# Mamba-2 scan and an ELU layer pair on one core: the first two blocks' second layer half in seven products

## Chip, cores, metric

One core of one Trainium2 chip runs the program. The metric is the device time of one execution in microseconds (us); for the kernel before it is the median of three runs, 355.29 us (355.22 to 355.34).

## The reference

All of it is float32. First a chunked state-space scan (Mamba-2 SSD) for 4 batches and 8 heads over 768 tokens, head size 32, state size 16; its output is laid out as 3072 tokens by 256 features and goes through two dense layers with an ELU between:

```python
# per chunk of tokens: cum = running sum of log(a)
M = (C @ B.T) * exp(cum_i - cum_j) * causal
y = M @ x + (C @ state) * exp(cum_i)
state = exp(sum) * state + B.T @ (x * exp(cum_last - cum_j))
...
h = x @ w_in                                  # (3072, 256) @ (256, 2048)
g = np.where(h > 0.0, h, np.exp(np.minimum(h, 0.0)) - 1.0)
out = g @ w_out                               # (3072, 2048) @ (2048, 256)
```

The weights arrive as float64 and are made into float32 words on the chip.

## The kernel before, in words

The 3072 tokens are cut into twelve blocks of 256 (`BLK`), numbered n = 0 to 11. Blocks 2k and 2k+1 form a pair: the same third of the sequence, in two batches. For every block the scan makes `yT` (features on partitions, tokens along the free axis). The first layer, `l1(n, i)`, makes 256 of the 2048 features (two chunks j of 128, index m = 2i + j) in one PSUM bank; `elu` turns that into a tile `g_of[n, i]` of 128 x 2 x 256: ScalarE does relu(-h) and the exponential, VectorE the last step. The second layer sums over m = 0 to 15 in PSUM.

From block 4 on, pairs go through both layers by Strassen's scheme in Winograd's form: a 2x2 block product by seven products instead of eight, for sums and differences of quarters. In layer one these are `front`, `mid` and `back` (products at L733) with `sum_y` (four differences of `yT`, GpSimd, L728). In layer two it is the generator `second(n)` (L820 to L900), which takes the pair n, n+1 in two halves of four indices i. Each `next` of it issues two products of 128 columns (L856); after each of the seven products a few operations follow: copies by ScalarE (L863, L875), additions into `c_sum` (`add`: by VectorE where an operand is in PSUM, else by GpSimd, L834), and in-place subtractions on the quarters of g (`sub`, GpSimd, L798). The operands are named as in the scheme: b11, b21, b12, b22 are quarters of g (`quarters`), t1 = b12 - b11 is put in b12's place (`sum_t1`, L810), t2 = b22 - t1 goes into a tile of its own (`sum_t2`). The weights have sums too: for each index i, `weight_steps` (L703) makes s3 = a11 - a21, then a21 + a22 in place, s2 and s4, for `w_in` (`s_in`) and for `w_out` (`s_out`).

In the kernel before, blocks 2 and 3 go through layer one plainly and through layer two by `second(2)`. Blocks 0 and 1 go through both layers plainly: `l2(n, j)` (L775) does, for the features m = 2j and 2j+1, one product of 256 columns for each of two halves of the tokens (L782), and behind the last one ScalarE copies the sum into the tile `ob` (L788), which is stored (L790).

The order of the work is written out by hand; every engine runs its own instructions in the program's order, and semaphores join them. The parts in order:

- a start-up, in which the scan of blocks 0 and 1, the first weights and `l1(0, 0..3)` are done;
- twelve steps s (L1040): `l1` of blocks 1 and 0 in turn, with the scan of block 2 and five pieces of the weights put in between (`w_take`: ScalarE and VectorE; `w_give`: VectorE, and GpSimd at L239);
- loops `n = 2` and `n = 3` (L1164), eight steps i each: `l2(n - 2, i)` and `l1(n, i)`, with the scans of blocks 3, 4 and 5 (`scan_ahead`, `turn_part`, `end_of_two`), the last pieces of the weights (n = 2), and the sums of the weights with t1 of block 2 (n = 3, `more_sums`, L1158). At i = 6 of `n = 3`, `across` and `inside` finish the scan of blocks 4 and 5 and `sum_y(4)` follows;
- loops n = 4, 6, 8, 10 over pairs: `front`, `mid`, `back` of pair n between the steps of `second(n - 2)`;
- `second(10)` alone.

A block's matrix of C is masked by heads in `mask_heads(n)` (L452, one VectorE operation of 128x512), between the transposes (`turn_square`, VectorE, L447) and `scores`. PSUM has seven buffers of one bank for everything (`ps_a`) and one for sums (`ps_o`). `c_sum`, the tile that collects the output of a pair, has one buffer, and so has the scratch `p_sum`; g has twelve buffers for even and twelve for odd n; t2 has four. All output and nearly all input goes through SP's DMA queue.

Of the kernel before, what the change touches and what calls it, by code (L numbers as in the profile page):

```python
# [16 lines left out]
P = 128  # L17
# [11 lines left out]
def kernel(  # L29
# [422 lines left out]
    def mask_heads(n):  # L452
        s = st[n]
        s["ctm"] = att.tile([P, 2, 2, P], F32, tag="ctm", name="ctm")
        nc.vector.tensor_tensor(
            out=s["ctm"], in0=s["ct"].unsqueeze(2).to_broadcast([P, 2, 2, P]),
            in1=hmask2.unsqueeze(1).unsqueeze(3).to_broadcast([P, 2, 2, P]), op=ALU.mult)
# [194 lines left out]

    def l1(n, i, parts=1):

        ps = psum([P, 2, BLK], "ps_h")
        for j in range(2):
            m = 2 * i + j
            for part in range(parts):
                toks = slice(part * BLK // parts, (part + 1) * BLK // parts)
                for k in range(KC):  # L660
                    nc.tensor.matmul(  # L661
                        out=ps[:, j, toks], lhsT=w_in[:, k, m * P:(m + 1) * P],
                        rhs=yT[n // 2][:, k, n % 2].rearrange("p u i -> p (u i)")[:, toks],
                        start=(k == 0), stop=(k == KC - 1))
        lag.append((n, i, ps))
# [107 lines left out]
    o_of = {}  # L773

    def l2(n, j, half=None):  # L775


        if j == 0 and half != 1:
            o_of[n] = p_o.tile([P, 2, DM], F32, tag="o", name="ps_o")
        for m in (2 * j, 2 * j + 1) if half is None else (2 * j + half,):  # L780
            for ts in range(2):
                nc.tensor.matmul(  # L782
                    out=o_of[n][:, ts], lhsT=g_of[n, j][:, m % 2, ts * P:(ts + 1) * P],
                    rhs=w_out[:, m], start=(m == 0 and ts == 0), stop=(m == MC - 1),
                    skip_group_check=True)
        if j == MC // 2 - 1 and half != 0:
            ob = ffn.tile([P, 2, DM], F32, tag="ob", name="ob", bufs=1)
            nc.scalar.copy(out=ob, in_=o_of.pop(n))  # L788
            r0 = row_of(n)
            nc.sync.dma_start(  # L790
                out=out[r0:r0 + BLK, :].rearrange("(t p) e -> p t e", p=P), in_=ob)
# [5 lines left out]
    def sub(out, in0, in1):  # L797
        nc.gpsimd.tensor_tensor(out=out, in0=in0, in1=in1, op=ALU.subtract)  # L798

    def quarters(n, i):  # L800


        A, B = g_of[n, i], g_of[n + 1, i]
        if n < 4:
            return A[:, 0], A[:, 1], B[:, 0], B[:, 1]
        return A[:, 0], B[:, 0], B[:, 1], A[:, 1]
# [5 lines left out]
    def sum_t2(n, half):  # L812
        for i in range(4 * half, 4 * half + 4):
            t2_of[n, i] = ffn.tile([P, BLK], F32, tag="t2", name="t2", bufs=4)
            b11, b21, b12, b22 = quarters(n, i)
            sub(t2_of[n, i], b22, b12)

    c_of = {}

    def second(n, last=False):  # L820


        c = c_of[n] = ffn.tile([P, 2, 2, 2, P], F32, tag="c", name="c_sum", bufs=1)
# [3 lines left out]
        for half in range(2):  # L827
# [8 lines left out]
            for r, a in enumerate((a11, a12, s1, s2, s3, a22, s4)):  # L836
# [25 lines left out]
                if r == 0:  # L862
                    nc.scalar.copy(out=p1, in_=ps)  # L863
                    for i in chunk:
                        b11 = quarters(n, i)[0]
                        sub(b11, t2_of[n, i], b11)
                    if half:
                        add(c11, c11, p1)
# [171 lines left out]
    for s, (n, i) in enumerate((  # L1040
            (1, 0), (1, 1), (1, 2), (0, 4), (1, 3), (0, 5), (1, 4), (0, 6), (1, 5), (0, 7),
            (1, 6), (1, 7))):
        l1(n, i, parts=2 if s < 2 else 1)
# [54 lines left out]
    def scan_ahead(n, i):  # L1098
# [29 lines left out]
        if 4 <= m < NP and n % 2 == 1:  # L1128
            if i == 0:
                scaled(m, nc.gpsimd)  # L1130
                scaled(m + 1, nc.gpsimd)
            for k in (i,) if m == 4 else (i, i + 1) if i % 2 == 0 else ():
# [25 lines left out]
    def more_sums(i):  # L1158
        sum_weights(nc.vector, a_out, s_out, i)
        sum_weights(nc.gpsimd, a_in, s_in, i)  # L1160
        sum_t1(2, i, nc.vector)


    for n in (2, 3):  # L1164
        for i in range(8):
            if n == 3 and i > 0:
                more_sums(i - 1)
            l2(n - 2, i)
            piece = todo < len(pieces) and (n, i) != (2, 1)
            if n == 2 and i == 0:  # L1170
                elu()
            if piece:
                w_take(todo, nc.scalar if i > 1 else nc.vector)
# [12 lines left out]
            if n == 2:  # L1186
# [3 lines left out]
                if i == 1:  # L1190
                    scores(3)
                    sums(3)
                    for q in range(4):
                        weigh(3, q)
                if i == 2:
                    states(3)
                if i == 6:
                    inside(across(3), 3)
            else:
                if i == 0:  # L1200
                    s_in[:], s_out[:] = weight_sums(), weight_sums()
            scan_ahead(n, i)
            end_of_two(n, 2 * i + 1)
    sum_t2(2, 0)
    left = weight_steps(nc.vector, a_out, s_out, 7)

    for n in range(4, NP, 2):
# [14 lines left out]
        for k in range(16):  # L1222
            i = k // 2
            if k % 2 == 0:
# [12 lines left out]
                else:  # L1237
                    front(n, i)
                    front_sums(n, i)
                    next_elu()  # L1240
                    l2s(2)
# [11 lines left out]
            else:  # L1253
                mid(n, i)
                if i == 0 and n > 4:
# [9 lines left out]
                if n == 4 and i < 4:  # L1265
                    next(left)()
                    if i == 0:
                        sum_weights(nc.gpsimd, a_in, s_in, 7)
                        sum_t1(2, 7)
# [45 lines left out]
```

## Time and profile before

| | us |
|---|---|
| median of three runs | 355.29 |
| the profiled execution | 354.71 |
| its span in the profile | 352.9 |
| TensorE busy | 346.8 (98% of the span) |
| VectorE busy | 240.5 (68%) |
| GpSimd busy | 231.7 (66%) |
| ScalarE busy | 204.2 (58%) |

The profile is of one execution; its span begins with the first instruction seen and ends with the last. PE is TensorE (PEld its weight loads, which run beside its products), DVE VectorE, ACT ScalarE, POOL GpSimd, SP the engine that issues most DMAs. A line of a timeline reads: start, duration, engine, line of the code, operation, output tile <- input tiles, shape, and in brackets the idle time just before it and what ended it. Consecutive instructions of one kind are merged, with their count behind "x"; the durations of TensorE's records overlap, so the cost of one is read from the start of one group to the start of the next. Costly groups of the work that the change touches:

| group | count | mean ns |
|---|---|---|
| L782 TensorE, layer two plain, 128x256 (two records a product) | 128 | 382 |
| L856 TensorE, seven products, 128x128, w_out with g (two records a product) | 640 | 275 |
| L455 VectorE, mask of C, 128x512 | 9 | 922 |
| L798 GpSimd, subtraction, 128x256 (three groups) | 120 | 730 to 752 |
| L810 GpSimd / VectorE, t1, 128x256 | 33 / 7 | 727 / 488 |
| L834 GpSimd, add, 128x256 | 30 | 725 to 728 |
| L834 VectorE, add from PSUM, 128x256 | 59 | 417 to 422 |
| L709 GpSimd, a step of the sums of w_in, 128x128 | 32 | 490 to 528 |
| L709 VectorE, a step of the sums of w_out, 128x128 | 32 | 433 to 469 |
| L728 GpSimd, a difference of yT, 128x256 | 16 | 734 to 752 |

### The profile page before, as it was taken

What the parts mean: (1) busy time and instruction counts of PE and PEld (TensorE: products, weight loads), DVE (VectorE), ACT (ScalarE), POOL (GpSimd) and SP (SyncE); (2) the same over time, 40 slices, a digit from 0 to 9 for tenths busy, and PEclk for the clock granted to TensorE, in tenths of its full rate; (3) what the DMA queues carried; (4) which work ended last, traced back from release to release, by engine and by line L of the source; (5) the groups of instructions that cost most, each with busy time, mean ns of one, the idle gap of its engine ahead of it and who ended that gap; (6) DMA issues with size and microseconds to landing.
All of it is one profiled execution on the core that took longest, in us unless ns stands there. A gap on an engine that the chain in (4) does not pass through costs nothing.

```text
span 352.9 us, 9967 instructions
## 1 busy us (share of the span) xinstructions
PE 346.8 (98%) x3958; PEld 312.8 (89%) x3958; DVE 240.5 (68%) x500; ACT 204.2 (58%) x496; POOL 231.7 (66%) x368
## 2 busy tenths in 40 slices
PE   8889999999999999999999999999999999999996
PEld 5568888888888999999999999999999999999996
DVE  4998979863999768684777684677684565656212
ACT  5869989787335677536677535586635444435100
POOL 5654554553576996887377788468687545465883
PEclk9999999999999999999999999999999999999999
DMA  8979988641450500155500145600000100000001
GB/s 148 255 195 258 230 196 213 133 74 32 82 128 7 115 1 2 19 112 119 115 0 2 15 93 124 134 3 0 2 2 4 60 3 0 2 0 32 31 2 59
DMA packets 72726, 26.49 MB, mean 75 GB/s; under 512 B 57768, under 2 KB 67560, under 8 KB 72680
## 3 DMA queue, kind: packets, MB, share of 16 engines
q1 hardware_dynamic: 70360, 25.60, 31.8%
q8 instruction: 31, 0.51, 0.6%
q10 hardware_dynamic: 2320, 0.26, 0.5%
q14 instruction: 15, 0.12, 0.1%
HBM read 22.51 MB, written 3.34 MB: 73 GB/s over the span
## 4 chain that ended last, share of the span: by engine, by line
PE 95%; DVE 3%; ACT 1%; POOL 0%; issue 0%; DVEq 0%; POOLq 0%
PE ps_o L856 35%; PE ps_h L733 28%; PE ps_h L661 14%; PE ps_o L782 8%; PE ps_y L629 2%; PE ps_g L535 2%; PE ps_y L610 1%; PE ps_st L565 1%; PE ps_idle L254 1%; DVE g L683 1%; PE ps_o L842 1%; DVE M L544 0%; DVE mag L229 0%; ACT L L505 0%; PE ps_x L475 0%; PE ps_x L494 0%
## 5 line engine op out<-in xcount | busy, mean ns | idle before, releaser
L674 ACT ACTIVATE e<-ps_h 128x512 f32<-128x512 f32 x96 | 57.1, 594 | 91.3 <-DVE ps_h L758 49.3
L856 PEld LDWEIGHTS ps_o<-w_out,g 128*128 128x128 f32 x640 | 79.9, 192 | 2.9
L856 PE MATMUL ps_o<-w_out,g 128*128 128x128 f32 x640 | 80.9, 275 | 0.0
L683 DVE SCALAR_TENSOR_TENSOR g<-e,ps_h 128x512 f32<-128x512 f32 x96 | 65.1, 680 | 14.3 <-ACT e L681 13.7
L681 ACT ACTIVATE e<-e 128x512 f32<-128x512 f32 x96 | 60.9, 635 | 2.0
L661 PE MATMUL ps_h<-yT,w_in 128*128 128x256 f32 (+1 forms) x272 | 60.3, 370 | 1.1 <-POOL w_in L239 0.5
L810 POOL TENSOR_TENSOR g<-g 128x256 f32<-128x256 f32 x33 | 24.0, 727 | 54.9 <-DVE g L683 54.8
L661 PEld LDWEIGHTS ps_h<-yT,w_in 128*128 128x128 f32 x272 | 48.5, 190 | 8.4 <-POOL w_in L239 1.5
L515 ACT ACTIVATE L<-L,ncum 128x64 f32<-128x64 f32 x160 | 41.1, 338 | 0.2
L856 PE MATMUL ps_o<-w_sum,g 128*128 128x128 f32 x304 | 39.9, 275 | 0.0
L856 PEld LDWEIGHTS ps_o<-w_sum,g 128*128 128x128 f32 x304 | 38.5, 192 | 1.1
L766 DVE TENSOR_TENSOR ps_h<-ps_h,u_sum 128x512 f32<-128x512 f32 x32 | 22.3, 698 | 24.0 <-PE ps_h L733 23.7
L733 PE MATMUL ps_h<-yT,w_in 128*128 128x256 f32 x128 | 38.5, 383 | 0.0
L733 PE MATMUL ps_h<-y_sum,w_in 128*128 128x256 f32 x128 | 38.1, 380 | 0.0
L733 PE MATMUL ps_h<-y_sum,w_sum 128*128 128x256 f32 x128 | 38.1, 379 | 0.0
L520 POOL TENSOR_SCALAR_AFFINE_SELECT L<-L 64x512 f32<-64x512 f32 x40 | 28.0, 700 | 12.0 <-ACT L L515 10.7
L750 DVE TENSOR_TENSOR u_sum<-ps_h,u_sum 128x512 f32<-128x512 f32 x32 | 22.1, 690 | 15.1 <-ACT u_sum L743 11.0
L758 DVE TENSOR_TENSOR ps_h<-ps_h,u_sum 128x256 f32<-128x256 f32 x32 | 13.8, 433 | 25.6 <-PE ps_h L733 25.4
L782 PE MATMUL ps_o<-w_out,g 128*128 128x256 f32 x128 | 30.7, 382 | 0.0
L798 POOL TENSOR_TENSOR t<-g 128x256 f32<-128x256 f32 x40 | 28.8, 751 | 0.2
L798 POOL TENSOR_TENSOR g<-g,t 128x256 f32<-128x256 f32 x40 | 28.8, 752 | 0.3
L798 POOL TENSOR_TENSOR g<-t,g 128x256 f32<-128x256 f32 x40 | 27.9, 730 | 1.1 <-PE ps_o L856 1.1
(121 smaller groups left out, 536.9 us busy)
## 6 DMA issues: line engine op xcount, KB each, us to landing
L<-flat SPq DMA_DIRECT2D x20, 256.0 KB
w<-in_moe_w_out_dram SPq DMA_DIRECT2D x8, 512.0 KB
w<-in_moe_w_in_dram SPq DMA_DIRECT2D x7, 512.0 KB
xr<-in_x_dram SPq DMA_DIRECT2D x24, 128.0 KB
out_dram<-c_sum SPq DMA_DIRECT2D x9, 256.0 KB
bc<-in_B_dram SPq DMA_DIRECT2D x24, 64.0 KB
bc<-in_C_dram SPq DMA_DIRECT2D x22, 64.0 KB
ec<-flat_exp SPq DMA_DIRECT2D x10, 128.0 KB
```

Source lines behind the costliest of these rows:

```text
L515: nc.scalar.activation(L[:, h, u], L[:, h, u], ACT.Exp, bias=ncum[:, u, row:row + 1])
L520: nc.gpsimd.affine_select(out=part, in_=part, pattern=[[0, 4], [0, 2], [1, Q]], compare_op=ALU.is_ge, fill=0.0, base=0, channel_multiplier=-1)
L661: nc.tensor.matmul(out=ps[:, j, toks], lhsT=w_in[:, k, m * P:(m + 1) * P], rhs=yT[n // 2][:, k, n % 2].rearrange("p u i -> p (u i)")[:, toks],
L674: nc.scalar.activation(begun[0], lag[0][2], ACT.Relu, scale=-1.0)
L681: nc.scalar.activation(e, e, ACT.Exp, scale=-1.0)
L683: nc.vector.scalar_tensor_tensor(out=g_of[n, i], in0=e, scalar=1.0, in1=ps, op0=ALU.subtract, op1=ALU.max)
L733: nc.tensor.matmul(out=out, lhsT=lhsT, rhs=rhs, start=first, stop=True, skip_group_check=True)
L766: nc.vector.tensor_tensor(out=c2, in0=c2, in1=u[:, 0:2], op=ALU.add)
L782: nc.tensor.matmul(out=o_of[n][:, ts], lhsT=g_of[n, j][:, m % 2, ts * P:(ts + 1) * P], rhs=w_out[:, m], start=(m == 0 and ts == 0), stop=( ...
L798: nc.gpsimd.tensor_tensor(out=out, in0=in0, in1=in1, op=ALU.subtract)
L810: eng.tensor_tensor(out=b12, in0=b12, in1=b11, op=ALU.subtract)
L856: nc.tensor.matmul(out=ps[:, ts], lhsT=b[:, ts * P:(ts + 1) * P], rhs=a[:, i], start=(i == chunk[0] and ts == 0), stop=(i == chunk[-1]), s ...
```

## The change

Blocks 0 and 1 are made ready for the seven products in the second half of layer two (features 1024 to 2047, m = 8 to 15).

- In the twelve steps, `l1(1, 0..3)` come first, and the features i = 4 to 7 of both blocks are made together by `l1_two`: one product of 512 columns (both blocks' tokens) for each k. `g_of[0, i]` then holds the features 2i of both blocks and `g_of[1, i]` the features 2i + 1, and `quarters` reads them so.
- `l2` sums only m = 0 to 7 (four steps for each block, all in loop `n = 2`); ScalarE copies the sum into `c_sum` instead of `ob`. The second half runs as `second(0)`, with its second half alone, in loop `n = 3`: four `next` a step for i < 4, then three. Blocks 0 and 1 are stored from `c_sum` in loop 4.
- t1 (`sum_t1(0, 4..7)`) and t2 of these blocks are made by GpSimd in loop `n = 2`; after product one, two of the four subtractions go to VectorE.
- The sums of `w_out` for i = 4 to 7 move to loop `n = 2`, those for 0, 1, 2 stay in `n = 3`, those for 3 follow at the start of loop 4 (VectorE as before). Of the sums of `w_in` (GpSimd), the first step of each i goes to loop `n = 2` (`in_first`), the other three stay in `n = 3` (`in_rest`). `sum_t2(2, 0)`, which stood behind loop `n = 3`, now follows product five of `second(0)`.
- `scaled` of blocks 4 and 5 moves from the start of loop `n = 3` to the end of `n = 2`; both `decay` steps of block 5 in loop 3 come at i = 0.
- The masks of C from block 4 on are two ScalarE activations of 128x256 with a scale by partition, instead of one VectorE operation.

```diff
     def mask_heads(n):
...
+        if n > 3:
+            for k in range(2):
+                nc.scalar.activation(
+                    s["ctm"][:, :, k], s["ct"], ACT.Copy, scale=hmask2[:, k:k + 1])
+            return
...
+    def l1_two(i, j):
+        ps = psum([P, 2, BLK], "ps_h")
+        for k in range(KC):
+            nc.tensor.matmul(
+                out=ps, lhsT=w_in[:, k, (2 * i + j) * P:(2 * i + j + 1) * P],
+                rhs=yT[0][:, k].rearrange("p n u i -> p n (u i)"),
+                start=(k == 0), stop=(k == KC - 1))
+        lag.append((j, i, ps))
...
-        if j == MC // 2 - 1 and half != 0:
-            ob = ffn.tile([P, 2, DM], F32, tag="ob", name="ob", bufs=1)
-            nc.scalar.copy(out=ob, in_=o_of.pop(n))
...
+        if j == MC // 4 - 1:
+            if n == 0:
+                c_of[0] = ffn.tile([P, 2, 2, 2, P], F32, tag="c", name="c_sum", bufs=1)
+            nc.scalar.copy(
+                out=c_of[0][:, n].rearrange("p t e c -> p t (e c)"), in_=o_of.pop(n))
...
-        if n < 4:
+        if n == 2:
             return A[:, 0], A[:, 1], B[:, 0], B[:, 1]
+        if n == 0:
+            return A[:, 0], B[:, 0], A[:, 1], B[:, 1]
...
-        for half in range(2):
+        for half in range(2) if n else (1,):
...
                     nc.scalar.copy(out=p1, in_=ps)
+                    if not n:
+                        add(c11, c11, p1)
                     for i in chunk:
                         b11 = quarters(n, i)[0]
-                        sub(b11, t2_of[n, i], b11)
+                        sub(b11, t2_of[n, i], b11, nc.vector if n == 0 and i < 6 else nc.gpsimd)
...
-    for s, (n, i) in enumerate((
-            (1, 0), (1, 1), (1, 2), (0, 4), (1, 3), (0, 5), (1, 4), (0, 6), (1, 5), (0, 7),
-            (1, 6), (1, 7))):
-        l1(n, i, parts=2 if s < 2 else 1)
+    for s in range(12):
+        if s < 4:
+            l1(1, s, parts=2 if s == 0 else 1)
+        else:
+            l1_two(s // 2 + 2, s % 2)
...
+    steps = second(0)
     for n in (2, 3):
         for i in range(8):
-            if n == 3 and i > 0:
-                more_sums(i - 1)
-            l2(n - 2, i)
...
+            if n == 2:
+                l2(i // 4, i % 4)
...
+            else:
+                for _ in range(4 if i < 4 else 3):
+                    next(steps)
...
+                if i == 0:
+                    sum_t1(0, 4)
+                    sum_t1(0, 5)
...
+                if i in (3, 4):
+                    sum_t1(0, i + 3)
...
+                if i > 4:
+                    sum_weights(nc.vector, a_out, s_out, i - 1)
                 if i == 6:
+                    sum_weights(nc.vector, a_out, s_out, 7)
                     inside(across(3), 3)
+                if i in (5, 6):
+                    t2(0, 2 * i - 6)
+                    t2(0, 2 * i - 5)
+                    in_first(2 * i - 10)
+                    in_first(2 * i - 9)
+                if i == 7:
+                    for k in range(4, 8):
+                        in_first(k)
+                    scaled(4, nc.gpsimd)
+                    scaled(5, nc.gpsimd)
             else:
-                if i == 0:
-                    s_in[:], s_out[:] = weight_sums(), weight_sums()
+                if i > 0:
+                    in_rest(i - 1)
+                    sum_t1(2, i - 1, nc.vector)
+                if i in (1, 4, 6):
+                    sum_weights(nc.vector, a_out, s_out, (1, 4, 6).index(i))
...
-    sum_t2(2, 0)
-    left = weight_steps(nc.vector, a_out, s_out, 7)
+    left = weight_steps(nc.vector, a_out, s_out, 3)
...
-                if i == 0 and n > 4:
+                if i == 0:
                     store(n - 4, 0)
                     store(n - 4, 1)
...
-                if n == 4 and i < 4:
+                if n == 4 and i == 0:
                     next(left)()
-                    if i == 0:
-                        sum_weights(nc.gpsimd, a_in, s_in, 7)
-                        sum_t1(2, 7)
+                    next(left)()
+                    in_rest(7)
+                    sum_t1(2, 7)
```

## The prediction

> **What bounds the kernel now.** I read the page's slices first, then its chain of work that ended last, then the busy time by stage, then the rows of the two engines that meet where the change ends.
>
> ```profile
> PE   8889999999999999999999999999999999999996
> POOL 5654554553576996887377788468687545465883
> PEclk9999999999999999999999999999999999999999
> ...
> PE 95%; DVE 3%; ACT 1%; POOL 0%; issue 0%; DVEq 0%; POOLq 0%
> ```
>
> The granted clock is full in every slice, and the chain is TensorE. The second view gives busy time by stage; per engine it is us and, in brackets, instructions. My cuts are the twelve steps of blocks 0 and 1, loop `n = 2`, loop `n = 3`, loop `n = 4`, and the rest.
>
> ```profile
> 27.20:51.70 24.50, 24.49 (x285) 21.19 (x286) 21.75 (x46) 22.34 (x57) 12.70 (x17) 1.00 0.98 225
> 51.70:82.60 30.90, 30.90 (x294) 26.56 (x293) 22.82 (x44) 26.50 (x66) 15.16 (x19) 1.00 0.58 135
> 82.60:114.70 32.10, 32.10 (x434) 27.81 (x433) 27.10 (x63) 15.48 (x35) 20.85 (x40) 1.00 0.30 69
> 114.70:168.70 54.00, 54.00 (x644) 50.24 (x643) 37.50 (x78) 32.22 (x82) 45.15 (x73) 1.00 0.30 62
> ```
>
> The first two numbers are the stretch and TensorE's busy time: they are equal, so from 27 us on TensorE never stands still, and its waits in that stretch come back empty. Two things follow. A product taken away shortens the program in full, as long as nothing new makes TensorE wait; and relief on VectorE, ScalarE or GpSimd is worth nothing by itself. In loop `n = 3` (third line) VectorE is the busiest of the others (27.10), GpSimd (20.85) still has 11 us free.
>
> **TensorE's own work.** Prices come from TensorE's timeline and chain; each product of the code leaves two records there. Eight products of 128 columns ("PE ps_o L856 x16") take 1.78 us, 0.2225 each; four of 256 columns ("PE ps_o L782 x8") take 1.73 us, 0.432 each. A narrow product thus costs 51.5% of a wide one.
> - Second halves of layer two: 32 products of 256 go (two blocks, m = 8 to 15, two token halves), 13.82 us. In come 7 products x 4 chunks x 2 token halves = 56 of 128: 12.46 us. Gain 1.36.
> - `l1_two`: 32 products of 256 become 16 of 512. From the two prices, 0.0132 us of a product is fixed and the rest goes by columns, so this saves 16 x 0.0132 = 0.21. The one 512-column row is the idle product at 1.1 us, among rows at over twice today's price (512 and 384 columns took 3.35 us there), and measures nothing of this stream. Bounds 0 (columns alone count) and 0.42 (twice the fixed part); I take 0.21.
> - `parts=2` at the second of the twelve steps goes: 8 x 0.2225 - 4 x 0.432 = 0.05.
>
> Sum 1.62 us less on TensorE. A rule speaks against this: the Trainium skill, "TensorE: Matmul & The Clock Gate", section "Back-to-back issue gap", gives about 81 ns for a sustained matmul of 128 columns with its weight load and 131 for 512, so narrow ones are dear. By a straight line between these (an estimate from that page) 256 columns take 98 ns, and with two records to a product 56 narrow ones would cost 9.1 us against 6.3 for the 32 wide ones: a loss of 2.8. The trace has 111 and 216 ns per record in this very stream, and decides.
>
> **GpSimd's new work, and where it meets TensorE.** GpSimd gets for blocks 0 and 1: four t1, four t2, two of the four subtractions after product one (VectorE has the other two), four after product two, and five adds of 128x256. It loses nothing: the sums of `w_in` are only cut in two, the first of each four steps (`in_first`) now in `n = 2`, the other three (`in_rest`) in `n = 3`. So 19 operations at 0.70 (spacing of consecutive ones, four in 2.78) come in between 52 and 114 us, 13.3 us, and with them the four t2 of block 2, which used to stand behind loop `n = 3`. All of these lie ahead of one thing that TensorE needs: `sum_y(4)`, whose second result is the operand of the second product of `front(4, 0)`.
>
> ```profile
> 111.58 0.73 POOL L728 TENSOR_TENSOR y_sum<-yT 128x256 f32<-128x256 f32 x1 [2.20 <-ACT yT L646]
> 112.80 0.85 POOL L728 TENSOR_TENSOR y_sum<-yT,y_sum 128x256 f32<-128x256 f32 x1 [0.48 <-ACT yT L646]
> ...
> 114.55 0.59 PE L733 MATMUL ps_h<-yT,w_in 128*128 128x256 f32 x2
> 114.98 0.59 PE L733 MATMUL ps_h<-y_sum,w_sum 128*128 128x256 f32 x2
> ```
>
> GpSimd now waits 2.20 us for ScalarE's copies and is done at 113.65, 1.33 us before the product at 114.98. That is the whole cover. Afterwards, with the gain, the product is due at 114.98 - 1.62 = 113.36. I count GpSimd forward in its new order:
> - To the states' products `Sx`: the last weight piece is joined at 75.1 (0.6 later, since ScalarE's copy of block 0's half sum, 0.57, now precedes the later pieces). Behind it stand its own 1.24, four t2 2.8, eight `in_first` 3.4 to 4.2, two `scaled` 1.2, six selects 4.2, one add 0.7, six subtractions 4.2, two `in_rest` 2.9 to 3.5: done at 96.3 to 97.8. `Sx` is then released by VectorE, now at 98.38, afterwards near 98.7 (one t1 of 0.41 moves ahead of it, TensorE is 0.1 ahead): covered by 0.9 us or more, and `Sx` ends at 100.5.
> - From there: three adds 2.2, one more 0.7, four t2 2.8; four `in_rest`. A set of four such steps took 2.01 at 122.75 (VectorE idle beside it) and 2.33 at 100.15 (VectorE summing weights too), less the first step 1.48 to 1.75, times four 5.9 to 7.0. The first two `y_sum` 1.5. Together 13.1 to 14.2: ready at 113.6 to 114.7.
>
> So TensorE waits 0.2 to 1.3 us at `front(4, 0)`. I take 0.75, the middle: VectorE has three of its seven sets of weight sums left in this loop, but six adds and two subtractions more. What queues behind the waiting product is all of TensorE, so the whole wait counts. It comes once: behind `sum_y` GpSimd has 2.8 us of t2 and two first steps of the weights fewer than now, so the subtractions that now start at 119.95 start no later, and the third and fourth `y_sum` are wanted 2 us further on.
>
> **The rest, at nothing, with its cover.**
> - ScalarE's masks. Not in the trace; a strip of 128x256 lies between 0.37 (copy, L743) and 0.60 (128x512 activation, L674), so a block pays 0.74 to 1.2 for VectorE's 0.92; I take 0.74. The Trainium skill, "ScalarE: Activation LUTs", section "What ACT_TABLE_LOAD costs", has 280 + 0.833 N ns with a pointer operand, so an estimate of 0.49 each; no run here shows it. Worst place: between the relu of a `back` and the copy of the next `front`, in loops 6 and 8. The copy then ends 0.5 late (1.0 at the upper price) and VectorE's `u_sum` with it, about 0.7 ahead of the product of `mid` that overwrites what it reads. Without that cover: up to 0.3 at each of the two places. The gain on VectorE, 7.4 us in all, buys nothing.
> - `s_out` sums: 16 steps of 0.45 move from loop 3 to the end of loop 2, where VectorE idles 2.2 to 3.6 us a step (its waits for `e` there). First use is product three of `second(0)`, 5 us later.
> - VectorE's two subtractions and GpSimd's six are wanted at products five and six, some 9 us on; 4 us of slack on GpSimd by the count above.
> - PSUM: the products add a tile of the seven-buffer pool on every other product. The tile reused by product five is a `scores` tile, read by 96.5, wanted at 98.3.
> - The two copies of half sums take the place of the two copies into `ob` (0.57). Block 0's store leaves SP's queue at 82.12 and block 1's at 113.63, and both come back behind the loads of B and C, the four `L<-flat` (done issuing at 100.2) and one `ec`, when the last add of `second(0)` is done, near 112; behind them stand one `ec` and four loads of x, now issued from 114.07 to 118.27, no later than now. The stores hold the one buffer of `c_sum`: VectorE's first add of `second(2)`, now at 123.47, must wait till they land. They have 9 us for that; in loop 6 the stores are issued from 166.20 and the same add, at 177.17, waits for none.
>
> **Sum.** 1.62 - 0.75 = 0.87 us. The profiled execution took 354.71 (span 352.9 and 1.81 around it), so 353.84 by its own account. The median of the runs is 355.29, 0.58 above the profiled one; taken from there, **354.4**.
>
> **Rivals.**
> 1. *The cover holds.* GpSimd meets its date, because VectorE leaves it alone or `Sx` comes earlier; the full 1.62, up to 1.83 with `l1_two` at its better bound: 353.5 to 353.8. For it: the lower count misses the date by only 0.2. Against: each step of GpSimd is behind another with no idle time after `Sx`.
> 2. *The gain is eaten.* GpSimd at the slow spacing throughout, and half a us late at `Sx`: wait 1.3 to 2.3, time 355.0 to 356.0, the middle of it no change.
> 3. *Slower: GpSimd becomes the bound of loop 3.* Place: the same product of `front(4, 0)`. If its 38 us of nearly unbroken work from 75 on run a tenth longer than counted, which is less than the 16% between 2.01 and 2.33 for the same four steps, it loses 3.8 less the 0.9 of cover, 2.9 above the count: wait up to 3.6, time 357.3. It decides from a wait of 1.62; below that the change gains. I put this case at 356 to 357.
> 4. *It doesn't do what it says:* narrow products dearer in the alternation with the 256-column ones of `l1(3, i)`. Against: loops from 4 on alternate them so already at 1.78 for eight. I give it no share of its own.
>
> **Chances.** Forecast (wait 0.3 to 1.2, 353.9 to 354.9) 0.42; cover holds 0.23; eaten 0.17; slower 0.18. A measurement tells about 0.2%, 0.71 us, from no change. Faster by more than that: the cover's 0.23 and two thirds of the forecast, 0.51. Within: the forecast's rest and most of the eaten case, 0.30. Slower: 0.19. The range takes in the cover's case and most of the eaten one, leaving out part of the slower case: 353.5 to 356.0.
>
> **What would show it.** In the profile after: rows of 56 products at 0.22 and 16 of 512 at about 0.85; TensorE without idle time till loop 4, then one idle stretch before `ps_h<-y_sum,w_sum` released by GpSimd's `y_sum`, 0.2 to 1.3; `y_sum` following GpSimd's weight sums with no wait for ScalarE. An idle TensorE elsewhere in loops 2 or 3, or `Sx` released later than 99.5, would make this wrong.

## The result, and the profile after

The changed kernel takes **357.75 us** (median of six runs, 356.70 to 360.28); the kernel before, on the same chip, 355.33 (355.22 to 355.63). The ratio is 1.0074, interval 1.005 to 1.0097: slower, where the forecast was 354.4 and the range ended at 356.0. The profiled execution took 356.70, with a span of 355.0 (before: 354.71 and 352.9).

First the slices and the chain of the changed kernel's page.

```profile
PE   8889999999998899999999999999999999999996
POOL 5564554789979977788467687558697545465883
PEclk9999999999999999999999999999999999999999
...
PE 93%; DVE 4%; ACT 1%; POOL 1%; issue 1%; DVEq 0%
```

The chain is still TensorE with the full clock in every slice, but two slices near 115 us have an 8 that was a 9, and GpSimd's digits in slices 8 to 14 are 7 to 9, where 3 to 9 stood. The busy times by stage follow (TensorE, its weight loads, VectorE, ScalarE, GpSimd); the cuts are the same four stages, each at its own time in this execution.

```profile
27.50:51.90 24.40, 24.38 (x245) 14.88 (x245) 21.81 (x46) 22.37 (x58) 12.61 (x17) 1.00 0.88 212
51.90:82.70 30.80, 30.80 (x293) 26.44 (x292) 27.79 (x49) 27.51 (x69) 22.23 (x30) 1.00 0.66 149
82.70:116.90 34.20, 31.65 (x483) 28.54 (x481) 31.76 (x65) 18.38 (x43) 30.72 (x55) 1.00 0.35 79
116.90:171.30 54.40, 54.40 (x643) 50.64 (x644) 35.78 (x75) 31.49 (x82) 42.11 (x68) 1.00 0.27 54
```

In loop 3 TensorE's busy time is now 2.55 us short of the stretch. VectorE went from 22.82 to 27.79 in loop 2 and from 27.10 to 31.76 in loop 3: in the second it has hardly any free time. TensorE's waits name the one place (first line), and its timeline shows it:

```profile
PE ps_h L748 <- POOL y_sum L743: 2.6, 1, 2.6
```

```profile
113.75 0.59 PE L748 MATMUL ps_h<-yT,w_in 128*128 128x256 f32 x2
116.90 0.70 PE L748 MATMUL ps_h<-y_sum,w_sum 128*128 128x256 f32 x2 [2.55 <-POOL y_sum L743]
```

It is the product and the releaser that the prediction named. The same product had no wait before. GpSimd's side of it:

```profile
100.40 1.82 POOL L592 TENSOR_TENSOR Sx<-S_new,hmask 128x64 f32<-128x64 f32 x6 [1.54 <-DVE S_new L587]
...
108.34 0.73 POOL L853 TENSOR_TENSOR c_sum<-c_sum,p_sum 128x256 f32<-128x256 f32 x1 [0.30 <-DVE p_sum L853]
109.03 3.16 POOL L812 TENSOR_TENSOR t<-g 128x256 f32<-128x256 f32 x4
...
116.02 0.83 POOL L743 TENSOR_TENSOR y_sum<-yT,y_sum 128x256 f32<-128x256 f32 x1
```

`y_sum`'s second result is there at 116.85. GpSimd was free 1.54 us ahead of `Sx` and waited for VectorE's states, so the lateness begins on VectorE.

**Where the 2.1 us of span come from.** From the first product of the twelve steps to the last group of products: 27.17 to 348.11 before (320.94), 27.55 to 350.12 after (322.57). The start-up gave 0.38; it differs from execution to execution (27.2 to 29.2 over kernels whose start-up code is equal). Of the other 1.63, the wait is 2.55, and TensorE's own work became 1.18 less by the same stretch of `e1_late_rest` below, which has no wait (319.76). Of the last 0.26, 0.17 lies at the wait itself (the products on both sides of it start 3.15 us apart, in `e1_late_rest` 0.43) and the rest behind it.

### The profile page after: what moved, and what is told of

The parts are those of the page before. It is cut to its first block, busy times and chain, and to the rows that moved or that the text cites. A ratio compares the mean times of both kernels' runs of the same rounds, so it can differ in the third digit from the quotient of the medians.

```text
span 355.0 us, 10011 instructions
## 1 busy us (share of the span) xinstructions
PE 346.3 (98%) x3966; PEld 307.3 (87%) x3966; DVE 244.5 (69%) x500; ACT 210.1 (59%) x514; POOL 243.5 (69%) x387
## 4 chain that ended last, share of the span: by engine, by line
PE 93%; DVE 4%; ACT 1%; POOL 1%; issue 1%; DVEq 0%
PE ps_o L875 39%; PE ps_h L748 27%; PE ps_h L676 10%; PE ps_h L662 4%; PE ps_o L797 4%; PE ps_y L634 2%; PE ps_g L540 2%; PE ps_y L615 1%; PE ps_st L570 1%; PE ps_idle L254 1%; DVE sgn L214 1%; DVE mag L229 1%; DVE g L698 1%; PE ps_o L861 1%; DVE M L549 0%
## 5 line engine op out<-in xcount | busy, mean ns | idle before, releaser
L875 PEld LDWEIGHTS ps_o<-w_out,g 128*128 128x128 f32 x704 | 87.7, 192 | 3.1
L875 PE MATMUL ps_o<-w_out,g 128*128 128x128 f32 x704 | 89.0, 275 | 0.0
L826 POOL TENSOR_TENSOR g<-g 128x256 f32<-128x256 f32 x37 | 27.5, 746 | 59.3 <-DVE g L698 59.2
L676 PE MATMUL ps_h<-yT,w_in 128*128 128x256 f32 (+1 forms) x200 | 45.9, 374 | 1.1 <-POOL w_in L239 0.5
L875 PE MATMUL ps_o<-w_sum,g 128*128 128x128 f32 x336 | 44.3, 275 | 0.0
L875 PEld LDWEIGHTS ps_o<-w_sum,g 128*128 128x128 f32 x336 | 42.6, 192 | 1.3
L676 PEld LDWEIGHTS ps_h<-yT,w_in 128*128 128x128 f32 x200 | 35.7, 190 | 6.7 <-POOL w_in L239 1.9
L812 POOL TENSOR_TENSOR t<-g 128x256 f32<-128x256 f32 x44 | 31.3, 741 | 0.3
L812 POOL TENSOR_TENSOR g<-g,t 128x256 f32<-128x256 f32 x44 | 30.8, 732 | 0.3
L748 PEld LDWEIGHTS ps_h<-y_sum,w_sum 128*128 128x128 f32 x128 | 24.2, 190 | 6.2 <-POOL y_sum L743 3.0
```

What stands on the lines that cost most here:

```text
L676: nc.tensor.matmul(out=ps[:, j, toks], lhsT=w_in[:, k, m * P:(m + 1) * P], rhs=yT[n // 2][:, k, n % 2].rearrange("p u i -> p (u i)")[:, toks],
L748: nc.tensor.matmul(out=out, lhsT=lhsT, rhs=rhs, start=first, stop=True, skip_group_check=True)
L812: eng.tensor_tensor(out=out, in0=in0, in1=in1, op=ALU.subtract)
L826: eng.tensor_tensor(out=b12, in0=b12, in1=b11, op=ALU.subtract)
L875: nc.tensor.matmul(out=ps[:, ts], lhsT=b[:, ts * P:(ts + 1) * P], rhs=a[:, i], start=(i == chunk[0] and ts == 0), stop=(i == chunk[-1]), s ...
```

## Experiments

**Theory.** VectorE and GpSimd slow each other and VectorE, not counted as late, hands over the states too late; GpSimd's list to `sum_y(4)` then ends after its date. **Rivals:** GpSimd's own list is longer than counted whatever VectorE does; TensorE's new products are dearer; ScalarE's masks cost. All runs beside the kernel before on the same chip; "behind loop 3's start" counts from the first product of that loop (82.45 before, 82.71 after).

**e0_again.** The changed kernel, unaltered.

> The changed kernel once more, unaltered, to see where its spread (356.70 to 360.28 us in six runs, against 355.22 to 355.63 before) lies. Theory A (GpSimd is late at sum_y(4), and its lateness differs from run to run): the profile again has one idle stretch of TensorE after 27 us, before ps_h<-y_sum,w_sum, and a run slower than 356.7 by d has that stretch longer by about d than the 2.55 us of the first profile. Rival B (the spread lies elsewhere, in the start-up or in a lower granted clock): the stretch is 2.3 to 2.8 us again and the difference of the spans stands elsewhere.

357.74 us (357.04 to 358.92, ten runs), ratio 1.0053, interval 1.0027 to 1.0078. The profile again has a wait of 2.55 at the same product. This execution is 0.73 slower than the first profiled one with the same wait, and its first product of the twelve steps came 0.74 later (28.29 against 27.55), with a wait of 0.8 for VectorE's M in the start-up. So here the difference is the start-up's, as rival B had it.

**e1_late_rest.** Three of the `in_rest` go behind loop 3; two of them (i = 4 and 5) stood ahead of `sum_y(4)`, the third already stood behind it.

```diff
-                if i > 0:
+                if 0 < i < 5:
                     in_rest(i - 1)
+                if i > 0:
                     sum_t1(2, i - 1, nc.vector)
...
+    for i in (4, 5, 6):
+        in_rest(i)
     left = weight_steps(nc.vector, a_out, s_out, 3)
```

> The three steps of the w_in sums for i = 4, 5 and 6 go behind sum_y(4), where GpSimd has time; nothing else moves, no work is left out. GpSimd's two triples ahead of sum_y took 112.16 to 115.22 in the profile, 3.06 us. Theory A (GpSimd's queue ahead of sum_y is the whole loss): y_sum's second result comes at about 113.8 against a product due at 114.2, TensorE doesn't wait, and the time falls by 2.55 + 0.15 from the profiled 356.70, to 353.7 to 354.3 in every run, with a spread like that of the kernel before. Rival B (narrow products or ScalarE's masks cost the time, and the wait only shows it): TensorE stands as long somewhere else, or the time stays above 355.3.

**354.20 us** (353.85 to 354.69), ratio 0.9948, interval 0.9922 to 0.9974: faster than both kernels, though five of the ten runs lie above the 354.3 that was expected as the upper end. No wait is left on TensorE behind 27 us. GpSimd and TensorE at the place:

```profile
112.26 0.77 POOL L743 TENSOR_TENSOR y_sum<-yT 128x256 f32<-128x256 f32 x1
113.12 0.73 POOL L743 TENSOR_TENSOR y_sum<-yT,y_sum 128x256 f32<-128x256 f32 x1
```

```profile
113.86 0.59 PE L748 MATMUL ps_h<-yT,w_in 128*128 128x256 f32 x2
114.29 0.59 PE L748 MATMUL ps_h<-y_sum,w_sum 128*128 128x256 f32 x2
```

`y_sum` is ready at 113.85, 0.44 ahead of its product; `Sx` was as late as in the changed kernel (100.50). So the six weight steps of 3.0 us that stood there were not due, and the one wait held the whole loss: the changed kernel's work without it is a gain.

**e2_sum0_later.** VectorE's sums of `w_out` for index 0 leave the place ahead of the states.

```diff
-                if i in (1, 4, 6):
-                    sum_weights(nc.vector, a_out, s_out, (1, 4, 6).index(i))
+                if i in (3, 4, 6):
+                    sum_weights(nc.vector, a_out, s_out, (3, 4, 6).index(i))
```

> VectorE's four steps of the w_out sums for i = 0 move from step 1 to step 3 of loop 3, so behind the states; nothing is left out, GpSimd's order is the same. In the profile they took 92.72 to 95.67, and Sx was released 2.02 us later than in the kernel before (100.40 against 98.38). Theory A1 (over half of the wait comes from VectorE, which is late with the states): Sx is released about 1.3 us earlier (VectorE then waits for e at 94.7), GpSimd's idle time of 1.54 before it goes, the wait of 2.55 shrinks to 1.0 to 1.5, and the time falls to 355.2 to 355.7 from 356.7. Theory A2 (GpSimd's own work is the bound, whenever Sx comes): the wait stays above 2.2.

359.33 us (357.35 to 360.25), ratio 1.0076, interval 1.0046 to 1.0106: not faster; the outcome (355.2 to 355.7) missed. But the first half of the theory held. GpSimd's timeline:

```profile
100.19 1.82 POOL L592 TENSOR_TENSOR Sx<-S_new,hmask 128x64 f32<-128x64 f32 x6 [0.58 <-DVE S_new L587]
...
109.80 0.73 POOL L853 TENSOR_TENSOR c_sum<-c_sum,p_sum 128x256 f32<-128x256 f32 x1 [2.01 <-DVE p_sum L853]
```

`Sx` starts 16.57 us behind loop 3's start instead of 17.69, 1.1 earlier. More was not to be had there: ahead of the handover VectorE now waits 1.93 us for ScalarE's `e`. Then the four moved steps stand in front of VectorE's `p_sum`; GpSimd's next addition waits 2.01 us for that, and TensorE 0.56 at 109.87. The lateness was shifted from one handover to the next, since VectorE has no free time between (95.65 to 109.72); `y_sum` is ready 34.68 behind loop 3's start (after: 34.14).

**e3_mask_vector.** The changed kernel with all masks of C on VectorE again (`if n > NP` for `if n > 3`).

> All masks of C on VectorE again, as before the change; the rest as changed. Theory A1 (VectorE is late in loops 2 and 3): the masks of blocks 4 and 5, 0.7 to 1.2 us each, stand ahead of the states on a VectorE that had no idle time from 76 to 114 us, so Sx comes 1 to 2 us later, and the wait at y_sum grows to 3.5 to 4.5: 357.6 to 358.7 against 356.7 in the same sort of run. Rival B (ScalarE's masks are part of the loss): the time falls by 0.3 or more.

359.94 us (358.86 to 361.64, four runs), ratio 1.0108, interval 1.0047 to 1.0169. `Sx` starts 18.7 behind loop 3's start, 1.0 later than with ScalarE's masks. The wait is 2.84, less than the expected 3.5 to 4.5, as TensorE itself is held up twice on the way (0.26 and 0.29); the time is above the expected 357.6 to 358.7, and in the profiled execution the granted clock was 0.63 from 120 to 124 us, behind the wait. `e0_again` took 357.74 on the same chip. Relief of VectorE, worth nothing before, is worth something here.

**e5_fill.** Four steps of `second(2)`, eight products, go ahead of the waiting `front(4, 0)`.

```diff
+                    early = 4 if n == 4 and i == 0 else 0
+                    l2s(early)
                     front(n, i)
...
-                    l2s(2)
+                    l2s(2 - early // 2)
                     end_of_two(n, k)
-                    l2s(2)
+                    l2s(2 - early // 2)
```

> The first four steps of second(2), eight products that need nothing of sum_y(4), go ahead of front(4, 0) on TensorE; no work is left out and GpSimd's order is the same. They take 1.78 us. Theory A (TensorE waits there for GpSimd and for nothing else): the product that needs y_sum is due 1.78 us later, the wait falls from 2.55 to about 0.8, and the time to 354.9 to 355.5, with the granted clock at 1.00 through the next 8 us in every run. Theory C on the spread (an idle stretch of over 2.5 us sometimes costs the clock behind it: 0.74 and 0.63 of it granted from 120 to 124 us in the two last kernels): the spread of this kernel's runs is that of the kernel before and no run stands above 357. Rival B (the wait's length doesn't matter, something else costs 2 us): the time stays at 356.7 or above.

356.15 us (355.50 to 359.25), ratio 1.0005, interval 0.9976 to 1.0035: above the expected 354.9 to 355.5, and one of the ten runs, 359.25 with a mean clock of 0.99, is above the 357 that theory C allowed. The wait falls to 0.77, about the 1.78 of the eight products less:

```profile
116.72 0.70 PE L748 MATMUL ps_h<-y_sum,w_sum 128*128 128x256 f32 x2 [0.77 <-POOL y_sum L743]
```

A second wait, 0.51 for VectorE's `u_sum`, comes in at 118.80, which was not expected.

**e6_no_out_sums.** This kernel leaves VectorE's sums of `w_out` out altogether; the seven products take parts of `w_out` in their place. All else is the changed kernel.

```diff
-            yield lambda: eng.tensor_tensor(out=out, in0=in0, in1=in1, op=op)
+            if eng is nc.vector:
+                yield lambda: None
+            else:
+                yield lambda: eng.tensor_tensor(out=out, in0=in0, in1=in1, op=op)
...
-        s2, s3, s4 = s_out
+        s2, s3, s4 = a_out[:3]
```

> VectorE's sums of w_out (32 steps, 16 of them in loop 2 and 12 in loop 3) are left out altogether; second() multiplies by parts of w_out itself in their place, the same number and shapes of products. GpSimd's work is the same. Theory A1 (GpSimd is late because VectorE is late and slows it; its own work by my count needs 13.1 to 14.2 us from Sx's end to y_sum and Sx comes 16.4 us behind loop 3's start): Sx is released 16.0 to 16.5 us behind loop 3's first product (17.7 in the changed kernel, 15.9 in the one before), y_sum's second result comes 31.0 to 32.0 behind it (34.1), and the wait is 0 to 1.0: 354.0 to 355.2. Theory A2 (GpSimd's own added work is the whole loss): y_sum's result stays above 33.3 behind loop 3's start and the wait above 1.7.

355.24 us (354.71 to 356.04), ratio 0.9979, interval 0.9955 to 1.0002. GpSimd's list is unaltered, and yet:

```profile
99.06 1.82 POOL L592 TENSOR_TENSOR Sx<-S_new,hmask 128x64 f32<-128x64 f32 x6 [1.12 <-DVE S_new L587]
...
114.03 0.73 POOL L746 TENSOR_TENSOR y_sum<-yT,y_sum 128x256 f32<-128x256 f32 x1
```

`Sx` starts 16.57 behind loop 3's start and `y_sum` is ready 32.27 behind it, both a little later than expected (16.0 to 16.5, 31.0 to 32.0). From `Sx`'s end to the second `y_sum` it is 13.88 us; the prediction had 13.1 to 14.2. The wait is 0.92, inside the predicted 0.2 to 1.3. So with VectorE out of the way the count of GpSimd's list is right, and VectorE's sums make 1.6 of the 2.55.

**e7_before_masks.** The kernel before, with the masks on ScalarE as the only edit.

> The kernel before with one part of the change alone: the masks of C from block 4 on by ScalarE. The prediction costed it at nothing. All theories but one: the same time as before within 0.3 us, no wait of TensorE behind 27 us, each of the 16 activations 0.40 to 0.50. If ScalarE's masks are a cost of their own: slower by 0.3 or more, with a wait on u_sum or e in loops 6 and 8.

355.36 us (355.11 to 356.71), ratio 0.9984, interval 0.9959 to 1.001, no new wait: nothing, as predicted.

**e8_before_wide.** The kernel before, with `l1_two` and the layout of g it needs, layer two plain.

```diff
+                g = g_of[m % 2, j][:, n] if n < 2 and j > 3 else g_of[n, j][:, m % 2]
...
-                    out=o_of[n][:, ts], lhsT=g_of[n, j][:, m % 2, ts * P:(ts + 1) * P],
+                    out=o_of[n][:, ts], lhsT=g[:, ts * P:(ts + 1) * P],
...
+    for s in range(12):
+        if s < 4:
+            l1(1, s, parts=2 if s == 0 else 1)
+        else:
+            l1_two(s // 2 + 2, s % 2)
```

> The kernel before with the products of 512 columns alone: features 4 to 7 of blocks 0 and 1 made together, layer two plain as before. The prediction gave 0.21 us for the 16 wide products and 0.05 for the one undivided step; the changed kernel's profile has 24.39 us from the first product of the twelve steps to the first of layer two, against 24.51. So 24.35 to 24.45 us in that stretch, and 0.1 to 0.3 us faster overall, with no wait of TensorE behind 27 us; 0.26 if the prediction was right.

366.33 us (366.05 to 370.86, five runs), ratio 1.0271, interval 1.0208 to 1.0335: 10.7 us slower, where 0.1 to 0.3 faster was expected. The profile is of the slowest of the five. The twelve steps take 24.36 us (before 24.51), so the wide products do save 0.15. The loss is elsewhere: TensorE stands still three times in the middle of `inside`, and no other engine's event ends it.

```profile
114.67 1.06 PE L629 MATMUL ps_y<-M,xr 64*32 64x64 f32 x51 [2.28 <-issue]
115.67 3.03 PE L793 MATMUL ps_o<-w_out,g 128*128 128x256 f32 x8
...
171.46 0.60 PE L629 MATMUL ps_y<-M,xr 64*32 64x64 f32 x36 [3.58 <-issue]
...
229.99 0.98 PE L629 MATMUL ps_y<-M,xr 64*32 64x64 f32 x58 [2.92 <-issue]
```

The four products behind the first one take 2.86 us instead of 1.83 (the same group in the kernel before); the granted clock was 0.77 from 116 to 120 us. A guess was that the place of these 128 small products in TensorE's own stream of instructions matters: the kernel has 40 records fewer than before ahead of them. The next two runs tested it.

**e9_before_narrow.** Order and layout of `e8_before_wide`, but each wide product as two of 256 columns, and `parts=2` for `s < 2`: as many TensorE instructions as before.

```diff
-        for k in range(KC):
-            nc.tensor.matmul(
-                out=ps, lhsT=w_in[:, k, (2 * i + j) * P:(2 * i + j + 1) * P],
-                rhs=yT[0][:, k].rearrange("p n u i -> p n (u i)"),
+        for n in range(2):
+            for k in range(KC):
+                nc.tensor.matmul(
+                    out=ps[:, n], lhsT=w_in[:, k, (2 * i + j) * P:(2 * i + j + 1) * P],
+                    rhs=yT[0][:, k, n].rearrange("p u i -> p (u i)"),
```

> The kernel before with block one's and two's second layer in the layout and order of e8_before_wide, but each 512-column product issued as two of 256 columns again, so that TensorE has as many instructions as in the kernel before. Theory P (the three issue waits of e8 come from where the dense stretch lies in TensorE's own instruction stream): no wait named issue inside loops 3, 4 and 6, and 355.2 to 355.7. Theory L (they come from the wide layout, its order of work or its buffers): the waits of 2 to 4 us remain, and near 366.

355.58 us (354.96 to 356.71), ratio 1.0, interval 0.9987 to 1.0014. None of the three waits.

**e10_wide_padded.** `e8_before_wide` with 20 products of two columns more at the very start.

```diff
+    for _ in range(20):
+        nc.tensor.matmul(
+            out=ps_idle[:, 0, 0:2], lhsT=idle, rhs=idle[:, 0:2], start=True, stop=True)
```

> e8_before_wide with 20 two-column idle products more at the very start of TensorE's stream, which shift everything behind them by 20 instructions and fall in the idle time of the start-up. Theory P (position in the instruction stream): the three issue waits of e8 vanish or stand at other products, and the time is 355.0 to 356 if they vanish. Theory L (layout or order): the same three waits at the same products, near 366.

364.39 us (361.82 to 364.94, six runs), ratio 1.0253, interval 1.0233 to 1.0274. The time alone would say "layout"; the profile, of the execution of 361.88, says otherwise. None of the three waits is there: the 128 products of `inside` run through in one group.

```profile
116.55 1.51 PE L632 MATMUL ps_y<-M,xr 64*32 64x64 f32 x128
117.99 1.99 PE L796 MATMUL ps_o<-w_out,g 128*128 128x256 f32 x8
```

From the first product of the twelve steps (34.30) to the last group (355.25) it is 320.95 us, as before (320.94). The padding itself made the start-up 7.1 us longer, against the expectation that it would fall in idle time: its 40 records take 5.28 us. Layout and order alone do not make the three waits: `e9_before_narrow` has both, and the changed kernel has the wide products too, and neither has such a wait. That speaks for the position in TensorE's stream, but it is not shown alone. In this run everything also comes 7.1 us later, and four of its six executions, with a mean clock of 1.0, took 364.3 to 364.9, some 2.5 us more than the profiled one and its like (361.8, clock 0.99); they have no profile, and why they are longer stays open. What in the chip makes the waits is not shown either.

**e11_longer_wait.** The changed kernel with four of GpSimd's subtractions done twice ahead of `sum_y(4)`.

```diff
                         sum_t2(n + 2, 0)
+                        if n == 0:
+                            for i in range(4):
+                                b11, b21, b12, b22 = quarters(2, i)
+                                sub(t2_of[2, i], b22, b12)
```

> The changed kernel with four of GpSimd's subtractions for block two's first half done twice, ahead of sum_y(4): some 2.8 us more on GpSimd (four of about 0.7), so TensorE's wait for y_sum becomes 2.55 + 2.8 = 5.3. If only the wait counts, 356.7 + 2.8 = 359.5. Theory C (a wait of this length is followed by a lower granted clock, worth 1.6 to 1.9 us, in nearly every execution rather than in some of them): 360.5 to 362, with a granted clock below 0.95 in the 8 us behind the wait.

362.38 us (361.8 to 362.93, four runs), ratio 1.0189, interval 1.0168 to 1.021. The timeline and the busy time in cuts of 4 us (the granted clock is the third number from the end):

```profile
120.75 1.22 PE L748 MATMUL ps_h<-y_sum,w_sum 128*128 128x256 f32 x2 [5.33 <-POOL y_sum L743]
121.77 1.06 PE L748 MATMUL ps_h<-y_sum,w_in 128*128 128x256 f32 x2
122.62 3.18 PE L875 MATMUL ps_o<-w_out,g 128*128 128x128 f32 x16
```

```profile
116.00:120.00 4.00, 0.00 (x0) 0.00 (x0) 1.11 (x2) 0.55 (x2) 3.61 (x9) 0.79 0.71 163
120.00:124.00 4.00, 3.25 (x11) 2.89 (x12) 1.03 (x3) 0.00 (x0) 3.62 (x7) 0.50 0.44 72
124.00:128.00 4.00, 4.00 (x26) 3.85 (x26) 1.62 (x3) 1.17 (x3) 3.63 (x7) 0.85 0.00 0
```

The time is a little above the expected 360.5 to 362. From the first product of `front(4, 0)` to the first one behind the second group of 16, it is 16.95 us here (114.83 to 131.78) and 12.05 in the changed kernel (113.75 to 125.80): 4.90 more, of which 2.78 is wait and 2.12 the lower clock. This wait cost more than its length.

## Why the prediction was wrong

- **The failing step** is the place of VectorE in the count of GpSimd: "`Sx` is then released by VectorE, now at 98.38, afterwards near 98.7". It was released at 100.40. Behind loop 3's start that is 17.69 against the predicted 16.5 (98.7 less 82.19, the start after a gain of 0.26). The step took one t1 of 0.41 as all that moves ahead, and "16 steps of 0.45 move from loop 3 to the end of loop 2, where VectorE idles 2.2 to 3.6 us a step" as free. These two views, of the kernel before and of the changed one, give least, median and greatest duration (ns) of VectorE's weight sums:

```profile
L709 DVE TENSOR_TENSOR w_sum<-w_out x16: 274/430/700, 88.6 to 134.1; 128x128 f32<-128x128 f32 x16
```

```profile
L724 DVE TENSOR_TENSOR w_sum<-w_out x16: 428/553/1055, 77.1 to 123.7; 128x128 f32<-128x128 f32 x16
```

  The median rose from 430 to 553; what made the steps longer (GpSimd is busier beside them) no run isolates. The 16 moved steps took 9.96 us where 7.2 was counted, and the last of them ended at 88.69, 6 us into loop 3. The idle time was used up, and VectorE runs from 76.5 to 114 us without a pause. These lists, again before and after, show what the handover met:

```profile
94.30 0.69 DVE L683 SCALAR_TENSOR_TENSOR g<-e,ps_h 128x512 f32<-128x512 f32 x1 [0.51 <-ACT e L681]
...
98.03 1.79 DVE L582 SCALAR_TENSOR_TENSOR S_new<-S_new,ec,ps_st 128x64 f32<-128x64 f32 x6
```

```profile
92.72 0.81 DVE L724 TENSOR_TENSOR w_sum<-w_out 128x128 f32<-128x128 f32 x1
...
95.67 0.67 DVE L698 SCALAR_TENSOR_TENSOR g<-e,ps_h 128x512 f32<-128x512 f32 x1
...
100.04 1.80 DVE L587 SCALAR_TENSOR_TENSOR S_new<-S_new,ec,ps_st 128x64 f32<-128x64 f32 x6
```

  Four sums of `w_out` at 92.72 to 95.67, 2.95 us where 1.8 was counted, stand in front of the `elu` of 95.67 (before: 94.30, with 0.51 idle ahead of it), which stands in front of M and the states (100.04; before: 98.03). `e2_sum0_later` (these four moved: `Sx` 1.1 earlier) and `e6_no_out_sums` (all left out: the same 16.57, as good as the predicted 16.5, and a wait of 0.92) show it.
- **GpSimd from `Sx` to `y_sum`**: 14.63 us (102.22 to 116.85) against 13.1 to 14.2, 0.30 of it a wait for VectorE's `p_sum`; without VectorE's sums 13.88. The count was right for a GpSimd beside which VectorE sums no weights. Ahead of `Sx` GpSimd's list ended at 98.86 instead of 96.3 to 97.8, but that was still covered, by the 1.54 it then waited.
- **The due date** was later than thought, 31.64 behind loop 3's start (114.35) instead of 31.17, since TensorE gained less. The sum closes: 0.75 + 1.18 (the states) + 0.98 (14.63 less the middle, 13.65) - 0.47 = 2.44, measured 2.55.
- **TensorE's gain** was 1.18, not 1.62. In `e1_late_rest` the 56 narrow products of loop 3 take 12.75 us, 0.2277 each: eight in a row 1.78 as predicted, but the groups right behind the scan's small products 0.1 more (95.32 to 97.21 for eight). The 32 wide ones that stood in loop 3 before show the same there (94.70 to 96.53 for four, 1.83) and took 14.01 instead of 13.82, so the products alone gained 1.26. The scan's own small products between them took 0.20 more than before (1.87 and 2.40 against 1.79 and 2.28). Loop 3 as a whole gained 1.06 (32.10 to 31.04) instead of 1.36. Four 512-column products take 3.43 instead of 3.40, and the twelve steps 24.39 instead of 24.51: 0.12 for `l1_two` and `parts` together instead of 0.26. The trace's rows were right against the page named there: no run shows narrow products as dear as its rule made them.
- **Rival 3** is what happened: "GpSimd becomes the bound of loop 3", at this product, "It decides from a wait of 1.62"; its wait was near (2.55 of "up to 3.6"), its cause half right: GpSimd's part behind `Sx` ran 7% over the middle of the count, and the other 1.18 came from VectorE's late handover. Its times (356 to 357, at most 357.3) were too low, since it kept the full gain of 1.62. Deciding point by the measured gain: 1.2.
- **Masks**: one takes 0.496 us (the estimate from the page was 0.49) and two, which overlap, 0.89 together (predicted 0.74), and they cost nothing (`e7_before_masks`). "The gain on VectorE, 7.4 us in all, buys nothing" held for the kernel before and failed for the changed one (`e3_mask_vector`).
- **The rest** (PSUM tiles, stores, later subtractions) held: TensorE waits nowhere else.
- **What is left over.** The profiled difference behind the start-up, 1.63, put on the median before, 355.29, gives 356.9; the measured median is 357.75. In `e0_again` such a rest was the start-up's; two of the six executions (359.42 and 360.28) have a mean clock of 0.995 and no profile. So some 0.8 us of the miss is not traced.

## What to carry to other kernels

Relief and load on an engine with idle time are free only until its list closes up: after adding work, count each engine's list to the next handover, not its share, and take durations from rows where both neighbours are as busy as they will be. When a long chain ends in a date, first look for work in it that isn't due; moving two weight sums (3.0 us) behind the date turned a loss of 0.7% into a gain of 0.5%. An alteration of a few TensorE instructions came with three waits elsewhere in its stream (`e8_before_wide`), so a change is judged by its waits and not by its time alone.

## What was not expected of the hardware

- **The clock was lower behind waits shorter than 3 us, in part of the executions.** In `e2_sum0_later`, with a wait of 2.55, the executions split in two: mean granted clock 0.999 or 1.0 with 357.35 to 358.03 us (four), 0.994 or 0.995 with 359.22 to 360.25 (six), some 2.0 apart. The profiled one is of the second kind, with the clock at 0.83 and then 0.74 behind the wait:

```profile
116.00:120.00 4.00, 1.64 (x5) 1.34 (x6) 1.02 (x2) 0.90 (x3) 3.84 (x7) 0.83 0.74 168
120.00:124.00 4.00, 4.00 (x25) 3.90 (x24) 1.89 (x4) 0.37 (x1) 3.76 (x7) 0.74 0.41 63
```

  Behind the 2.84 of `e3_mask_vector` it was 0.95 and then 0.63. It does not come each time: the same wait of 2.55 has the full clock behind it in the profiles of the changed kernel and of `e0_again`. The mean clock of an execution does not say where it was lowered. The changed kernel's 359.42 and 360.28 have 0.995, its other four runs 1.0 or 0.999; with no wait (`e1_late_rest`) ten of ten are at 0.999 or above, with 5.33 four of four are below 1. But in `e0_again` six of ten have 0.995 and hardly differ in time, with the profiled dip (0.79 and 0.78 from 12 to 20 us) in the start-up, and the kernel before, which has no such wait, has 0.99 or 0.995 in five of 63. The Trainium skill, "TensorE: Matmul & The Clock Gate", Part 1 on the clock gate, puts the clock back after an idle window of about 3.4 us; here a lower clock followed idle times of 2.28 (`e8_before_wide`) and 2.55 in the profiled executions.
- **A lower clock behind products of two columns, in one profile.** Behind the 40 two-column records of `e10_wide_padded` (4.25 to 9.53 us) the granted clock was 0.53 from 8 to 12 us and 0.62 from 12 to 16, with TensorE's records busy all the time; in the kernel before it was 1.00 there. Four of the six executions have a mean clock of 1.0, so this too does not come each time, and that the small products are the cause is not shown.
- **TensorE can wait for nothing that the profile shows**, 2.28 to 3.58 us inside a dense run of small products. With 20 products more ahead of them the profiled execution had no such wait; what makes them is open.
